# A fused attention and gated-convolution kernel: the order of all its steps and loads written anew

## The chip, the core and the metric

The kernel runs on one core of one Trainium2 chip. A core has five engines that run side by side, each working through its own instructions strictly in the order in which the program issued them: TensorE (PE in the profile: matrix products and transposes into PSUM), VectorE (DVE), ScalarE (ACT, the exponentials, ReLU and tanh), GpSimd (POOL) and SyncE (SP). SP computes nothing here; it issues nearly all transfers, and they go through one hardware queue that is served by the core's 16 DMA engines. Engines wait for each other, and for transfers, through semaphores. The metric is the device time in microseconds (us) of one execution, the median of several runs.

## What is computed

Eight sequences of 576 positions go through an attention with 8 heads of width 64 and a decay, and the result through a feed-forward network with a gate made from a convolution over three neighbouring positions. All inputs and the output are float32.

```python
def _attn_ref(q, k, v, f):                      # q, k, v: (8, 8, 576, 64), f: (8, 8, 576)
    scores = scale * np.matmul(q, k.transpose(0, 1, 3, 2))
    cum = np.cumsum(np.log(np.clip(f, 0.0001, 1.0)), axis=-1)
    decay = cum[:, :, :, None] - cum[:, :, None, :]
    scores = np.where(causal, -1000000000.0, scores + decay)
    attn = np.exp(scores - np.max(scores, axis=-1, keepdims=True))
    attn = attn / (np.sum(attn, axis=-1, keepdims=True) + 1e-09)
    return np.matmul(attn, v)

def _moe_ref(x, w_in, conv_w, w_out):           # x: (8, 576, 512), d_ff = 1024
    h = np.maximum(x @ w_in, 0.0)
    conv_out = sum(conv_w[k] * hp[:, k:k + S, :] for k in range(3))
    return (h * (1.0 / (1.0 + np.exp(-conv_out)))) @ w_out
```

## The kernel before

The work is cut into steps with short names. Attention goes by **blocks** of four heads, so that there are 16 blocks, 0 to 15, two for each sequence; the feed-forward part goes by sequence, 0 to 7. In the names below `hb` is a block, `b` a sequence, `i` a pair of heads (two in a block, `i` = 2`hb` and 2`hb`+1), and `ff` one of eight slices of 128 hidden columns.

Loads, all issued by SP unless said otherwise:
- `ld0.*` and `ld1.*` bring q and k of blocks 0 and 1 in plainly; TensorE then transposes them (`tp`, nine 128x128 transposes each, L166) and ACT or DVE copies them from PSUM into place (`cl0`, `cl1`, L172 and L174).
- `q{hb}.0` and `q{hb}.1` bring q and k of every later block in with a transposing transfer each (L180), into one of four places in turn (`qk_85` holds blocks 0, 4, 8, 12, `qk_86` blocks 1, 5, 9, 13, and so on). Up to block 7 DVE then clears the rows that carry the decay (`cl{hb}.side`, L186), and `rw{hb}` (L204, L205; SP or ACT issues it) copies these rows in from `image`, which `ki` has written from the sums of log f (`dca`, `dcl`, `dcs`, `dck`). From block 8 on `fi{hb}` fills them.
- `v{b}.0` to `v{b}.4` bring v of a sequence (L211); `va{hb}.0` and `va{hb}.1` cast it to 16 bits for a block (L219, L221; POOL, ACT or DVE). `va{hb}.0` needs `v{b}.0` to `v{b}.3`.
- `wi0` to `wi3` and `wo0` to `wo3` bring the weights (L518); `wic`, `woc` cast them.

Attention: `sd{i}`, `so{i}.0`, `so{i}.1` and `st{hb}` are the scores (L314; the mask is added on TensorE by L322 in blocks 0 to 7), `ed`, `eo` and `et` their exponentials on ACT (L355, L372, L334). `pv{hb}.0` and `pv{hb}.1` multiply by v (L391, L396), `n` and `m` divide by the sum on DVE (L405, L407), `t` transposes the result on TensorE (L416) and `tx` copies it (L419). In block 0 the decay is added by two more products for each score (L317, L319).

Feed-forward: `f{b}.{ff}` is the first product (L431), `r` its ReLU on ACT (L442), `c` and `d` the convolution on DVE (L448, L450), `a` the tanh on ACT (L453), `g` the gate on DVE (L460), `o{b}.{c}` the second product (L476), `e` the copy out of PSUM and `s` the store (L503 and its neighbours; L498 in the last sequence).

PSUM is four banks of 128x1024, handed out in turn: a step on TensorE that takes a bank waits until the step that empties the bank's last content has ended. So each score product waits for an exponential some steps back.

What sets the order is a table, `ORDER`: a string with the name of every step (and of the engine where a step can run on more than one, as in `va2.0@ACT`). The program issues the steps in that order, so it fixes the order on each engine and on the transfer queue; the scheduler moves nothing. A step's resources (PSUM banks, buffers) go first come, first served along the same table. Eight semaphores are used in turn for transfers, so that the ninth transfer is issued only when the first of the nine has arrived.

## Time and profile before

| | |
|---|---|
| median of three runs | 247.25 us (245.05, 247.81 and 247.25) |
| span of the profiled execution, first to last instruction | 244.7 us |
| TensorE busy | 228.6 us, 93% of the span |
| ScalarE busy | 206.8 us, 85% |
| VectorE busy | 205.5 us, 84% |
| GpSimd busy | 51.9 us, 21% |
| moved by the DMA engines | 49.68 MB, mean 203 GB/s |

The profile page gives for the profiled execution its span alone; what lies around a span (the start and the end of an execution) is in the runs' times and not in it, so the median stands 2.55 us above the span. "Busy" counts overlapping instructions of an engine once. Two tenths-rows of the page show that TensorE is full in nearly every fortieth of the span but the first ten and the last, and that the DMA engines are full until about five sixths of it.

### The profile page before, as it was taken

How to read it: one execution, taken by the hardware profiler on the slowest of the kernel's cores; microseconds unless marked ns; L12 is line 12 of the kernel's file. 1: busy time of each engine (PE TensorE's matmuls, PEld its weight loads, DVE VectorE, ACT ScalarE, POOL GpSimd, SP SyncE). 2: the span in 40 equal slices, each digit the busy share in tenths (PEclk: the TensorE clock that was granted, in tenths of full speed). 3: DMA queues.
4: the chain of work that ended last, by engine and by line, in shares of the span. 5: the costliest groups of instructions: out<-in, count | busy, mean ns of one | idle time of the engine just before them, and what ended most of it. 6: DMA issues, size and time to landing. Idle time of an engine off the chain costs nothing.

```text
span 244.7 us, 6393 instructions
## 1 busy us (share of the span) xinstructions
PE 228.6 (93%) x2627; PEld 146.1 (60%) x2627; DVE 205.5 (84%) x324; ACT 206.8 (85%) x278; POOL 51.9 (21%) x77
## 2 busy tenths in 40 slices
...
GB/s 189 334 169 250 278 184 189 223 198 306 196 216 196 169 182 220 238 268 251 224 212 274 194 198 269 270 102 196 265 198 227 195 209 4 106 173 77 171 85 216
DMA packets 120424, 49.68 MB, mean 203 GB/s; under 512 B 109879, under 2 KB 110647, under 8 KB 120395
## 3 DMA queue, kind: packets, MB, share of 16 engines
...
q10 hardware_dynamic: 322, 0.47, 0.6%
q8 instruction: 20, 0.33, 0.6%
...
HBM read 21.11 MB, written 10.17 MB: 128 GB/s over the span
## 4 chain that ended last, share of the span: by engine, by line
PE 81%; DMA 5%; DVE 5%; ACT 5%; issue 1%; SPq 1%; ACTq 0%; DVEq 0%
PE ps L476 26%; PE ps L431 23%; PE ps L314 15%; PE ps L391 7%; DMA qk<-image 3%; PE ps L322 3%; PE ps L396 3%; DMA u<-in_f_dram 2%; PE ps L416 2%; ACT qk L172 2%; DVE u L450 2%; DVE u L448 1%; ACT ht L442 1%; ACT pp L372 1%; PE ps L317 1%
## 5 line engine op out<-in xcount | busy, mean ns | idle before, releaser
L431 PE MATMUL ps<-xt,w_in_f 128*128 128x512 f16 (+1 forms) x512 | 71.0, 288 | 0.4 <-DVE xt L419 0.4
L372 ACT ACTIVATE pp<-ps 128x1024 f16<-128x1024 f32 x64 | 64.8, 1032 | 3.7 <-PE ps L314 2.3
L476 PE MATMUL ps<-w_out_f,hg 128*128 128x512 f16 x288 | 66.8, 379 | 0.0
L314 PE MATMUL ps<-qk 128*128 128x128 bf16 (+2 forms) x576 | 63.9, 241 | 2.1 <-DMA qk<-image 0.9
L448 DVE SCALAR_TENSOR_TENSOR u<-ht,cwt 128x576 f32<-128x576 f16 x64 | 52.4, 832 | 4.4 <-ACT ht L442 4.2
L450 DVE SCALAR_TENSOR_TENSOR u<-ht,cwt,u 128x576 f32<-128x576 f16 x64 | 53.9, 856 | 0.5
L453 ACT ACTIVATE hg<-u,cw 128x576 f16<-128x576 f32 x64 | 48.7, 782 | 6.1 <-DVE u L450 6.0
L431 PEld LDWEIGHTS <-w_in_f 128*128 128x128 f16 x512 | 34.7, 99 | 29.4 <-issue 1.3
L314 PEld LDWEIGHTS <-qk 128*128 128x128 bf16 x576 | 39.4, 98 | 19.2 <-issue 2.5
L442 ACT ACTIVATE ht<-ps 128x576 f16<-128x576 f32 x64 | 41.0, 664 | 6.4 <-PE ps L431 2.8
L476 PEld LDWEIGHTS <-hg 128*128 128x128 f16 x288 | 26.9, 98 | 28.9
L460 DVE SCALAR_TENSOR_TENSOR hg<-hg,ht 128x576 f16<-128x576 f16 x51 | 38.6, 767 | 0.6 <-ACT hg L453 0.5
L358 POOL TENSOR_SCALAR_AFFINE_SELECT pp<-pd 128x1024 f16<-128x1024 f32 x16 | 19.7, 1244 | 53.6 <-ACT pd L355 53.6
L391 PE MATMUL ps<-va,pp 128*128 128x65 f16 x640 | 25.3, 194 | 1.7 <-DVE va L219 1.7
L391 PEld LDWEIGHTS <-pp 128*128 128x128 f16 x640 | 23.0, 98 | 4.2 <-DVE va L219 1.9
L407 DVE TENSOR_TENSOR xm<-ps,rc 128x896 f16<-128x896 f32 (+1 forms) x32 | 23.9, 751 | 0.5
L355 ACT ACTIVATE pp<-ps 128x1024 f16<-128x1024 f32 x16 | 16.6, 1038 | 5.2 <-PE ps L314 4.0
L219 POOL CAST va<-vf 128x1024 f16<-128x1024 f32 x8 | 10.0, 1247 | 34.3 <-PE ps L314 18.8
L355 ACT ACTIVATE pd<-ps 128x1024 f32<-128x1024 f32 x16 | 16.2, 1023 | 1.2 <-PE ps L314 0.5
L405 DVE RECIPROCAL rc<-ps 128x14 f32<-128x14 f32 (+1 forms) x32 | 6.6, 207 | 10.2 <-PE ps L396 4.9
L322 PE MATMUL ps<-mask,ident 128*128 128x512 bf16 (+1 forms) x40 | 14.4, 364 | 0.4 <-ACT pp L372 0.3
L481 ACT COPY ob<-ps 128x1024 f32<-128x1024 f32 (+1 forms) x14 | 12.9, 918 | 0.3 <-issue 0.2
...
## 6 DMA issues: line engine op xcount, KB each, us to landing
...
```

Of the source, the lines that this page charges most:

```text
L314: nc.tensor.matmul(o, tk[:, h * S + k0:h * S + k0 + 128], tq[:, h * S + q0:h * S + q0 + n], start=first, stop=last and not by_matmul(hb, h))
L355: nc.scalar.activation(o, ps_of(f"sd{i}").rearrange("p (s c) -> p s c", s=2), AF.Exp, scale=SCALE)
L372: nc.scalar.activation(pair(i)[:, s, 512:1536], ps_of(f"so{i}.{s}"), AF.Exp, scale=SCALE)
L391: nc.tensor.matmul(ps[:, c:c + D + 1], block(hb, h, m, n), va[:, h, m, 0:D + 1], start=(m == 0), stop=(m == n))
L407: nc.vector.tensor_tensor(xm[:, CUT * D * u:CUT * D * u + nj * k * D].rearrange("p (j x d) -> p j x d", x=k, d=D), got[:, :, :, 0:D], r.un ...
L431: nc.tensor.matmul(ps[:, t0:t1], w_in_f16[:, cc, 128 * ff:128 * (ff + 1)], xt[:, cc // 2, x:x + t1 - t0], start=(cc == 0), stop=(cc == NCC ...
L442: nc.scalar.activation(ht_of(b, ff)[:, 2:2 + S], ps_of(f"f{b}.{ff}")[:, 0:S], AF.Relu, scale=1.0 if (b, ff) in LATE else 0.5)
L448: nc.vector.scalar_tensor_tensor(u, ht[:, 1:1 + S], cwt[:, ff, 0:1], ht[:, 2:2 + S], op0=ALU.mult, op1=ALU.add)
L450: nc.vector.scalar_tensor_tensor(u, ht[:, 3:3 + S], cwt[:, ff, 1:2], u, op0=ALU.mult, op1=ALU.add)
L453: nc.scalar.activation(hg_of(b, ff), u_t[slot[f"c{b}.{ff}", "u"]], AF.Sigmoid if (b, ff) in LATE else AF.Tanh, scale=cw[:, ff, 1:2])
L460: nc.vector.scalar_tensor_tensor(hv, hv, 1.0, ht_of(b, ff)[:, 2:2 + S], op0=ALU.add, op1=ALU.mult)
L476: nc.tensor.matmul(ps[:, 512 * j:512 * (j + 1)], w, w_out_f16[:, ff, :], start=(ff == 0), stop=(ff == NFF - 1))
```

## The change

One string is replaced: `ORDER`. The names in it are the same 1056 steps; their order is new on every engine and on the transfer queue, and some steps that may run on either of several engines have another one. The rest of the program is untouched (its lines move down by 51, since the new table is broken into lines).

```diff
 ORDER = """
-dca cw ld0 ld1 ld0.0.0 tp0.0.0 dcl ld0.1.0 ld0.0.1 tp0.0.1 tp0.1.0 v0.0 ld0.1.1 ld1.0.1 ld1.0.0 dcs dck v0.1 ...
+ld0 v0.0 dca q2.0 ld1 dcl q2.1 ld0.0.0 ld0.0.1 tp0.0.0 cl0.0.0@ACT tp0.0.1 ld1.0.0 dcs cl2.1 ld1.0.1 dck cl0.0.1@DVE
+ki@ACT cw v0.3 tp1.0.0 cl1.0.0@ACT ld0.1.0 tp1.0.1 tp1.1.0 v0.2 ld0.1.1 cwt v1.0 wi1 v0.4 cl1.0.1@DVE tp1.1.1 v1.4 sd0
...
 """
```

Steps with another engine: `ki` and `rw3` go to ACT's queue, `rw4` and `rw5` to SP's; `va2.0` goes from DVE to ACT, `va3.0`, `va3.1` and `va4.0` from ACT to POOL, `va5.0` and `va6.0` from POOL to DVE, and more than twenty further casts, copies and stores change places in the same way.

Three places of the order matter below. The first is the start of SP's queue. Before, q and k of block 0 come first (`hg` is where the plain loads land):

```order
L159 DMA hg<-in_q_dram 128x576 x2
L159 DMA hg<-in_k_dram 128x576
L211 DMA vf_89<-in_v_dram 128x8x64
L159 DMA hg<-in_k_dram 128x576
L159 DMA hg<-in_k_dram 128x2x576
L159 DMA hg<-in_q_dram 128x2x576
L211 DMA vf_89<-in_v_dram 128x8x64 x3
```

Now a load of v and both transposing loads of block 2 (`qk_87`) stand ahead of them, and the plain loads of block 1 (128x2x576) stand ahead of the second half of block 0's:

```order
L262 DMA vf_89<-in_v_dram 128x8x64
L231 DMA_TRANSPOSE qk_87<-in_q_dram 128x2304
L231 DMA_TRANSPOSE qk_87<-in_k_dram 128x2304
L210 DMA hg<-in_q_dram 128x576
L210 DMA hg<-in_k_dram 128x576
L210 DMA hg<-in_q_dram 128x2x576
L210 DMA hg<-in_k_dram 128x2x576
L262 DMA vf_89<-in_v_dram 128x8x64
L210 DMA hg<-in_q_dram 128x576
```

So the first scores of block 0 have more in front of them on the queue, and block 2 is there early. The second place is ScalarE between the exponentials of block 1 and the first ReLU. Before it has no cast there (`pp` and `pt` are exponentials, `ht` is a ReLU):

```order
L372 ACTIVATE pp_99<-ps_131 128x1024
L355 ACTIVATE pp_100<-ps_131 128x2x512
L442 ACTIVATE ht_115<-ps_130 128x576
L442 ACTIVATE ht_116<-ps_132 128x576
L372 ACTIVATE pp_100<-ps_129 128x1024
```

Now a cast of v (`va2.0`, from `vf_90`, which waits for the four large loads of sequence 1's v) and the issue of block 3's row copies (`rw3`) stand ahead of two exponentials of block 2 and of the first ReLU:

```order
L385 ACTIVATE pt_103<-ps_131 128x256
L270 CAST va_94<-vf_90 128x4x4x64
L423 ACTIVATE pp_99<-ps_130 128x1024
L255 DMA qk_88<-image 1x2304
L256 DMA qk_88<-image 2x2304
L423 ACTIVATE pp_100<-ps_129 128x1024
L493 ACTIVATE ht_115<-ps_131 128x576
L423 ACTIVATE pp_100<-ps_130 128x1024
```

Before, that cast was on VectorE, behind the first convolutions. The third place is SP's queue around blocks 4 to 6 (`qk_85` is block 4, `qk_86` block 5, `qk_87` block 6). Before, the loads of block 6 follow three weight loads and all of sequence 2's v:

```order
L180 DMA_TRANSPOSE qk_86<-in_q_dram 128x2304
L180 DMA_TRANSPOSE qk_86<-in_k_dram 128x2304
L518 DMA ob_125<-in_moe_w_out_dram 128x2x512
L518 DMA ob_126<-in_moe_w_out_dram 128x2x512
L518 DMA ob_127<-in_moe_w_out_dram 128x2x512
L211 DMA vf_89<-in_v_dram 128x8x64 x2
L211 DMA vf_89<-in_v_dram 64x8x64
L211 DMA vf_89<-in_v_dram 128x8x64 x2
L518 DMA ob_128<-in_moe_w_out_dram 128x2x512
L180 DMA_TRANSPOSE qk_87<-in_q_dram 128x2304
L180 DMA_TRANSPOSE qk_87<-in_k_dram 128x2304
```

Now they stand between the two loads of block 5, and the row copies of block 6 ahead of those of block 5:

```order
L231 DMA_TRANSPOSE qk_86<-in_q_dram 128x2304
L262 DMA vf_89<-in_v_dram 128x8x64 x2
L255 DMA qk_85<-image 1x2304
L256 DMA qk_85<-image 2x2304
L231 DMA_TRANSPOSE qk_87<-in_q_dram 128x2304
L231 DMA_TRANSPOSE qk_87<-in_k_dram 128x2304
L231 DMA_TRANSPOSE qk_86<-in_k_dram 128x2304
L262 DMA vf_89<-in_v_dram 128x8x64
L255 DMA qk_87<-image 1x2304
L256 DMA qk_87<-image 2x2304
```

TensorE's order follows: the first score product of block 6 (`sd13`) now stands ahead of that of block 5 (`sd11`), both ahead of the first sequence's second product, and far earlier among TensorE's steps than before.

More of the change, by code (lines that the diff above doesn't have):

```diff
@@ new lines @@
+ld0 v0.0 dca q2.0 ld1 dcl q2.1 ld0.0.0 ld0.0.1 tp0.0.0 cl0.0.0@ACT tp0.0.1 ld1.0.0 dcs cl2.1 ld1.0.1 dck cl0.0.1@DVE
+ki@ACT cw v0.3 tp1.0.0 cl1.0.0@ACT ld0.1.0 tp1.0.1 tp1.1.0 v0.2 ld0.1.1 cwt v1.0 wi1 v0.4 cl1.0.1@DVE tp1.1.1 v1.4 sd0
+cl1.1.1@DVE cl2.0 tp0.1.0 tp0.1.1 cl1.1.0@ACT so0.0 cl0.1.0@ACT rw1@SP wi2 ed0 rw2@SP v0.1 q3.1 so0.1 q3.0 cl0.1.1@DVE
+va0.0@POOL va0.1@DVE wic2@POOL cl3.1 v1.1 wi0 sd1 v1.2 so1.1 eo0.0 ed1 va1.0@DVE sd2 eo1.1 va1.1@POOL wi3 st0 eo0.1
+ed2 so1.0 so2.1 et0 sd3 v1.3 eo1.0 wic1@POOL eo2.1 ed3 so2.0 sd5 ed5 cl3.0 eo2.0 pv0.0 so3.1 pv0.1 wo1 n0.0 q4.0 m0.0
@@ new lines @@
+so3.0 eo3.1 n0.1 m0.1 wic0@POOL va3.0@POOL sd4 st1 eo3.0 pv1.0 et1 ed4 n1.0 st2 so5.0 pv1.1 et2 t0 m1.0 n1.1 m1.1
+va2.0@ACT t1 so4.1 eo5.0 tx0@DVE rw3@ACT so4.0 tx1@DVE q4.1 q5.0 cl4.0 eo4.1 f0.0 f0.1 f0.2 r0.0 wic3@POOL c0.0 eo4.0
+v2.0 d0.0 h0 r0.1 r0.2 f0.3 woc1@POOL cl4.1 a0.0 so5.1 c0.2 r0.3 eo5.1 f0.4 c0.3 va2.1@POOL r0.4 st3 sd6 et3 v2.2
+rw4@SP va3.1@POOL d0.3 c0.1 q6.0 ed6 sd7 c0.4 pv2.0 a0.3 ed7 so6.1 d0.4 f0.5 so6.0 n2.0 eo6.1 g0.0 m2.0 d0.1 pv2.1
+so7.0 r0.5 f0.6 n2.1 q6.1 a0.4 cl5.0 eo6.0 eo7.0 q5.1 so7.1 a0.1 m2.1 sd8 cl6.0 g0.4 d0.2 eo7.1 v2.1 r0.6 st4 cl6.1
@@ new lines @@
+pv3.0 so8.0 a0.2 et4 c0.5 ed8 n3.0 rw6@SP sd9 v2.3 g0.2 eo8.0 m3.0 wo2 pv3.1 so8.1 ed9 n3.1 d0.5 f0.7 eo8.1 m3.1 v3.0
+cl5.1 t2 r0.7 so9.0 t3 tx2@ACT c0.6 tx3@DVE c0.7 sd13 rw5@SP so9.1 g0.3 a0.5 eo9.0 eo9.1 ed13 g0.1 f1.0 v2.4
+va4.0@POOL sd11 wo0 d0.6 pv4.0 so11.1 r1.0 woc0@POOL f1.1 g0.5 n4.0 woc2@POOL ed11 sd10 eo11.1 m4.0 st6 f1.2 a0.6 v3.3
+wo3 c1.0 r1.1 va4.1@POOL d0.7 et6 ed10 c1.1 r1.2 pv4.1 n4.1 d1.0 h1 g0.6 woc3@DVE so10.1 q7.1 so11.0 d1.1 eo10.1 f1.3
+f1.4 eo11.0 r1.3 a0.7 m4.1 va5.0@DVE va5.1@ACT a1.1 q7.0 so10.0 g0.7 r1.4 a1.0 q8.0 cl7.0 g1.1 v3.2 cl7.1 v4.0 f1.5
@@ new lines @@
+r1.5 o0.0 t4 c1.4 c1.5 o0.1 c1.2 tx4@ACT d1.5 sd12 st5 v3.1 d1.4 eo10.0 ed12 et5 e0.0@ACT pv5.0 a1.4 n5.0 d1.2 rw7@SP
+m5.0 so13.0 pv5.1 f1.6 n5.1 eo13.0 g1.0 q8.1 m5.1 v4.4 f1.7 g1.4 v3.4 va6.0@DVE q9.1 st7 c1.3 a1.2 r1.6 d1.3 et7 r1.7
+sd14 so13.1 c1.6 c1.7 a1.5 so12.0 d1.7 eo12.0 o0.2 eo13.1 t5 so14.1 a1.3 zc g1.2 ed14 o0.3 tx5@DVE f2.0 f2.1 d1.6 q9.0
+eo14.1 e0.1@ACT r2.0 fi8 va7.0@DVE a1.6 so12.1 f2.2 g1.5 a1.7 r2.1 g1.3 g1.6 f2.3 va6.1@DVE sd15 r2.2 eo12.1 v4.3 v4.1
+va7.1@DVE r2.3 so15.0 fi9 v4.2 c2.1 c2.0 d2.1 so15.1 ed15 c2.2 eo15.0 f2.4 d2.0 g1.7 pv6.0 eo15.1 sd16 s0.1 n6.0 m6.0
```

33 lines of the change are left out of this document (32 added, 1 removed).

## The prediction

> **What bounds the kernel now.** I read the windows first (columns: stretch, its length, busy time and count of each engine, TensorE clock, DMA share, GB/s), then the end of the chain of waits (start, length, what).
>
> ```profile
> 0.00:60.00 60.00, 47.99 (x647) 36.16 (x647) 39.23 (x76) 43.60 (x52) 14.64 (x41) 0.97 1.03 232
> 60.00:240.70 180.70, 180.66 (x1992) 109.93 (x1986) 165.85 (x248) 162.88 (x226) 37.29 (x37) 1.00 0.88 194
> ...
> 228.58 12.10 PE ps L476 x56
> 240.71 0.38 ACT ob L492
> 241.11 0.42 DVE u L492
> ```
>
> From 60 us to the last product at 240.7 TensorE is busy for 180.66 of 180.70 us; what can be won lies in the first 60 us (12.0 us idle) and in the 4.0 us from 240.7 to the span's end at 244.7. To compare two orders I need the work itself, back to back. These rows of the chain and of the timeline give it:
>
> ```profile
> 15.78 0.50 PE ps L166 x9
> 195.77 1.96 PE ps L431 x16
> 197.73 0.44 PE ps L314 x4
> 202.10 1.00 PE ps L391 x32
> 206.07 0.44 PE ps L396 x20
> 212.11 3.45 PE ps L476 x16
> ...
> 45.06 0.38 PE L322 MATMUL ps<-mask,ident 128*128 128x512 bf16 x1
> 45.50 0.38 PE L322 MATMUL ps<-mask,ident 128*128 128x512 bf16 x1
> ```
>
> A transpose step is 0.50, `f` 0.98, `o` 1.73, `so` 0.44 (1.31 in block 0, three products for one), `pv.0` 1.00, `pv.1` 0.80 with its changes of shape, `sd` 0.88 with the mask (half of it from 45.06 to 45.50), 0.45 without it and 1.78 in block 0, `st` 0.1 to 0.45, `cw` 0.9. Over all steps: f 62.7, o 62.1, so 31.4, sd 23.1, st 2.9, pv 28.8, transposes 9.5, cw 0.9: about 221.6 us. I call **lag** the start of a step less the work ahead of it (these prices, added along TensorE's steps in the table); the span is 221.6 + last lag + 4.0.
>
> ```profile
> 7.15 0.98 PE L296 MATMUL ps<-one,pd 3*128 3x3 f32 x8 [7.15 <-DMA pd<-in_moe_conv_w_dram]
> 12.22 0.58 PE L322 MATMUL ps<-mask,ident 128*128 128x512 bf16 x1
> 37.30 0.65 PE L431 MATMUL ps<-xt,w_in_f 128*128 128x512 f16 x4
> 61.02 0.78 PE L416 MATMUL ps<-ident,xm 128*128 128x128 f16 x8
> ...
> PE ps L391 <- DVE va L219: 1.7, 1, 1.7
> ...
> 48.00:50.00 2.00, 0.33 (x4) 0.05 (x3) 2.00 (x4) 2.00 (x3) 0.00 (x0) 1.00 1.25 115
> 50.00:54.00 4.00, 4.00 (x44) 2.67 (x45) 3.62 (x7) 4.00 (x6) 0.00 (x0) 0.57 1.13 240
> ```
>
> Before, the lag is 9.3 at the first score (12.2 - 2.9 of work), 12.6 at `f0.0` (37.3 - 24.7), 18.3 at `t3` (61.0 - 42.75) and 19.1 at 228.58 (work ahead 221.6 - 12.1). The 5.7 us between `f0.0` and `t3` are 1.7 for a cast on VectorE (`va2.0`), 1.7 for half clock (0.57 over 4 us is 1.7 lost, right after that wait), and 2.3 of small waits.
>
> **The transfer queue.** It is what a new order has to live with. The SP rows give the time to issue a transposing load, which is the time in which the queue takes it:
>
> ```profile
> L180 SPq DMA_TRANSPOSE qk<-in_k_dram x14: 2011/2847/3962, 15.3 to 175.2; - x14
> 94.34 4.45 SPq L180 DMA_TRANSPOSE qk<-in_q_dram x2
> ...
> q8 instruction: 20, 0.33, 0.6%
> ...
> 29.00:30.00 1.00, 1.00 (x14) 0.75 (x13) 0.00 (x0) 1.00 (x2) 0.49 (x1) 1.00 1.63 297
> 30.00:31.00 1.00, 1.00 (x24) 0.81 (x24) 0.00 (x0) 1.00 (x2) 0.32 (x1) 1.00 1.91 104
> 31.00:32.00 1.00, 0.67 (x21) 0.33 (x17) 0.57 (x2) 1.00 (x2) 0.72 (x1) 1.00 0.21 44
> ...
> 9.00:10.00 1.00, 1.00 (x12) 1.00 (x11) 0.97 (x2) 0.99 (x2) 0.00 (x0) 1.00 1.06 396
> 13.00:14.00 1.00, 1.00 (x19) 0.88 (x17) 0.76 (x1) 0.37 (x1) 0.00 (x0) 1.00 1.23 211
> 24.00:28.00 4.00, 3.55 (x61) 2.83 (x61) 2.04 (x3) 2.18 (x4) 2.02 (x2) 1.00 0.86 266
> ```
>
> Two that were not stopped took 4.45, 2.2 each; the median is 2.85. There were 20 instruction fetches of 16 KB, one for some 128 of TensorE's 2627 products. Where one meets a transposing load, the queue falls from 297 to 104 and 44 GB/s: about 1.6 us lost in 30 to 32. Rates for the rest: plain q and k 396 GB/s (0.75 us for 0.295 MB, 1.5 for 0.59), v 211 (1.24 for 0.262 MB), weights 266 (1.97 for 0.524 MB).
>
> The Trainium skill, "Runtime: NRT & Kernel Launch", Instruction fetch mechanics, says that instructions come in blocks of 16 KiB through a queue of the sequencer's own and that this is mostly hidden. By that rule every transposing load would cost the 2.0 us of the shortest. The trace agrees on the blocks and not on the hiding: 44 GB/s.
>
> **The change, part by part.** All instructions are kept, so the 221.6 stay; an engine that is given another cast pays about 1 us off the path, since ScalarE and VectorE are busy for 163 and 166 of the 180.7 us.
>
> (1) The first score. The queue now holds, before the second load of block 1: v 1.24, two transposing loads 4.4, f 0.75, two plain loads 1.5, two large ones 3.0; with 1.8 to the first data and 1.0 to arrive (estimates, from the 2.1 us between the end of an SP issue at 20.90 and the VectorE step that waited for it), `ld0.0.0` is there at 9.9, `ld1.0.1` at 13.7. TensorE does `tp0.0.0` from 9.9 (0.93 each while the clock is low, as in the rows from 8.06), then `tp0.0.1`, `cw`, `tp1.0.0`, `tp1.0.1`, `tp1.1.0` until 14.7. `tp1.1.1` needs the bank that ScalarE empties with `cl1.0.0`, and ahead of that ScalarE has `cl0.0.0` and now the three issues of `ki`:
>
> ```profile
> 13.48 1.82 SPq L281 DMA_DIRECT2D image<-kc  x3
> L172 ACT ACTIVATE qk<-ps,lim 128x1152 uint16<-128x1152 uint16 x5 | 6.3, 1307 | 0.0
> L186 DVE TENSOR_SCALAR qk<-qk,lim 128x2304 uint16<-128x2304 uint16 x12 | 10.4, 879 | 1.1 <-DMA qk<-in_q_dram 1.1
> L407 DVE TENSOR_TENSOR xm<-ps,rc 128x896 f16<-128x896 f32 x16 | 17.4, 1087 | 0.3
> L219 ACT CAST va<-vf 128x1024 f16<-128x1024 f32 x4 | 4.3, 1068 | 0.0
> L372 ACT ACTIVATE pp<-ps 128x1024 f16<-128x1024 f32 x64 | 64.8, 1032 | 3.7 <-PE ps L314 2.3 <-PE ps L319 1.4
> ```
>
> 10.9 + 1.3 + 1.8 + 1.3 = 15.3, the turn until 15.8: `sd0` at 15.8 with 3.9 of work ahead, lag 11.9. Price: +2.6.
>
> (2) `f0.0`. On VectorE `cl3.0` stands ahead of `n0.0`, so block 0's division waits for block 3's load. Queue up to `q3.0`: 1.8 + 6.0 plain + 0.75 f + 7.45 v (five large, two half) + 3.95 (two weights) + 0.6 row copies + 8.8 (four transposing) + 2.1 (two fetches, one on a transposing load) = 31.45, there at 32.4. Then `cl3.0` 0.88, `n0.0` and `m0.0` 1.3, and behind that bank `sd4`, `pv1.0`, `so5.0`, `pv1.1`, its division, `t1`, `so4.1`: 39.9. ScalarE meanwhile stands at `va2.0`, which needs `v1.3`: 31.45 + three v 3.7 + two weights 3.95 + a fetch 0.5 + 1.0 = 40.6; cast 1.07, `eo5.0` 1.03, `so4.0` 0.44: `f0.0` at 43.1, work ahead 25.8, lag 17.3 (before 12.6). If `v1.3` were in time, 40.3 and 14.5. I take the first: every term is a row's. Price: +4.7, with the 2.6 of (1) in it.
>
> (3) From there to `t3`. The cast that cost 1.7 is done by then, the half clock is not certain (below), and of the 2.3 of small waits I keep half: block 3's `so7.0` still waits for `m2.0`, as its like did before. Lag 17.3 + 1.1 = 18.4, against 18.3.
>
> (4) Block 6 and 5. `sd11` needs the row copies of block 5; its work ahead is 48.0, before 50.6. The queue up to them: 1.8 + 6.0 + 0.75 + 17.4 (v: 13 large, two half) + 11.8 (six weights) + 1.5 (five row copies) + ten transposing loads at 2.2 = 22.0 + fetches 3.6 (one on a transposing load, four beside: by counting 128 products for each fetch, they now fall on weights and v) = 64.85, there at 65.9: the lag cannot be under 17.9. At the median of 2.85, which has its fetches in it, 22.8; at 2.0, 15.9. I take 2.2, the rows without a stop, because the counted fetches lie elsewhere. It ends just before (3) does, so it adds nothing, but it leaves no slack. Blocks 7 and 8 come out alike (17 to 18).
>
> (5) The rest. Before, the lag grew by 0.8 after `t3`; I keep that. At the end the last chunk is now copied whole (0.59 instead of two halves of 0.4) and stored whole: +0.2.
>
> **Sum.** Lag 18.4 + 0.8 = 19.2; 221.6 + 19.2 + 4.2 = 245.0, against 244.7 of the profiled span. With the 2.55 us by which the median stands above the span: 247.5.
>
> **Rivals.** *Faster: the loads come in time.* For it: transposing loads that are not stopped take 2.0 to 2.2, and in (2) the lag without the wait for `v1.3` is 14.5. With 2.0 and no fetch on a transposing load the limit of (4) is 14.8; 14.5 + 0.6 of small waits is 15.1, 3.2 under before's 18.3: 247.25 - 3.2 + 0.2 = 244.2, and down to 243 if the small waits go too. It decides if `v1.3` is there before 38 and block 5's rows before 63.5. Against it: the queue was never that fast for ten such loads in a row.
>
> *Slower: TensorE waits for block 5, 6, 7 or 8.* The queue keeps the median 2.85 of before, since a fetch that comes a few us later than planned falls on a transposing load after all (so the change would not do what it is made for). The lag at `sd11` is then 22.8, 4.5 above before: 247.25 + 4.5 + 0.2 = 252.0. It decides if block 5's rows come after 68.6 (lag 20.6). For it: the first needs of blocks 5, 6, 7 and 8 come 2.6, 21.7, 6.3 and 8.1 us of work earlier than before, so what slack the queue had is spent.
>
> *Half clock.* Before, a wait of 1.7 us in 48 to 50 is followed by 0.57 of the clock. The wait at `so4.0` in (2) is of that size, so 1.7 us may come back: time 249.2, inside my case. The Trainium skill, "TensorE: Matmul & The Clock Gate", Part 1, says that the clock falls to half after an idle window of about 3.4 us and stays there until a busy one; here a window that was only about half idle was enough.
>
> **Chances.** Within 1% (244.8 to 249.7; about what a measurement here can tell from no change): 0.42, my own case with its price of 2.1 to 2.5 for a transposing load, with or without half clock; its own range is 245 to 249.7. Faster by more: 0.33, the first rival, 243 to 244.8. Slower by more: 0.25. Leaving out one in ten at each end: 243.0 to 251.5.
>
> **What would show it.** (1) `sd0` near 15.8 and three DMA issues on ScalarE between its copies; wrong if it starts by 13. (2) A VectorE row that waits for `q3` ahead of block 0's division and a ScalarE cast (L270) that waits for v for 2 us or more; wrong if `f0.0` starts before 40. (3) No TensorE wait for a VectorE cast near 48. (4) GB/s falling below 100 in the windows of weights or v and not of transposing loads; waits of TensorE for `qk<-image` between 60 and 110 mean the slower rival. Wrong in sum if TensorE's idle time before 60 us is under 9 or if it idles by more than 2 us after 70.

## The result, and the profile after

| | before | after |
|---|---|---|
| median of the runs of this comparison | 246.64 us (four, 245.05 to 247.81) | 252.99 us (four, 252.71 to 254.18) |
| ratio | | 1.028, 95% interval 1.022 to 1.034 |
| span of the profiled execution | 244.7 us | 251.0 us |
| TensorE busy | 228.6 us | 227.8 us |
| lag (as the prediction defines it) at `sd0`, `f0.0`, `t3`, the last products | 9.3, 12.6, 18.3, 19.1 | 17.0, 18.7, 22.2, 24.0 |
| TensorE's last product to the span's end | 4.0 us | 5.1 us |

The changed kernel is 2.8% slower by the ratio, which is estimated from the single runs and is not the quotient of the two medians. Here and below, medians leave out executions that took over 1.5% longer than the fastest of their kernel. TensorE does the same work, and waits more. The windows of the changed kernel (the columns as before; the second ends with TensorE's last product at 245.9) say where:

```profile
0.00:60.00 60.00, 43.81 (x575) 33.57 (x576) 35.51 (x68) 38.10 (x45) 13.44 (x41) 1.00 1.10 227
60.00:245.90 185.90, 184.04 (x2056) 112.44 (x2053) 172.04 (x258) 167.16 (x233) 38.49 (x36) 1.00 0.87 188
```

In the first 60 us TensorE idles 16.2 us (12.0 before), in the rest 1.9 (none before). Most of the first part is one wait at the very start. The timeline of the changed kernel there (start, length, engine or its queue, line, operation; in brackets the idle time ahead and what ended it):

```profile
0.80 0.61 ACTq L275 DMA_DIRECT2D u<-in_f_dram  x1
0.80 0.46 SPq L262 DMA_DIRECT2D vf<-in_v_dram  x1
1.32 3.88 SPq L231 DMA_TRANSPOSE qk<-in_q_dram  x1
5.25 4.60 SPq L231 DMA_TRANSPOSE qk<-in_k_dram  x1
8.85 0.46 DVE L585 TENSOR_SCALAR u<-u 128x576 f32<-128x576 f32 x1 [4.58 <-DMA u<-in_f_dram]
9.89 0.58 SPq L210 DMA_DIRECT2D hg<-in_q_dram  x1
13.16 2.10 PE L217 MATMUL ps<-ident_b,hg 128*128 128x128 bf16 x18 [13.16 <-DVE kc L326]
18.04 3.06 PE L217 MATMUL ps<-ident_b,hg 128*128 128x128 bf16 x27 [0.77 <-DMA hg<-in_k_dram]
20.90 0.47 PE L373 MATMUL ps<-mask,ident 128*128 128x512 bf16 x1
```

The plain loads of block 0 are issued only at 9.89, when both transposing loads of block 2 have been taken; TensorE's first transpose starts at 13.16 (the row names a cast as the releaser, but what came is `hg`, issued at 9.89; the cast is no input of a transpose), the first score at 20.90. The transposes ahead of it follow each other at 0.107 us a product (27 in 2.86 us from 18.04) where later ones take 0.055. By the records of single packets the first transposing load ran from 3.7 to 9.0, 5.3 us. The windows show what the queue did in that time, in the changed kernel:

```profile
3.00:4.00 1.00, 0.00 (x0) 0.00 (x0) 1.00 (x5) 0.36 (x1) 1.00 (x11) 1.00 1.30 301
4.00:5.00 1.00, 0.00 (x0) 0.00 (x0) 0.27 (x2) 0.00 (x0) 0.88 (x13) 1.00 1.25 180
5.00:6.00 1.00, 0.00 (x0) 0.00 (x0) 0.00 (x0) 0.00 (x0) 0.78 (x4) 1.00 1.35 150
6.00:7.00 1.00, 0.00 (x0) 0.00 (x0) 0.00 (x0) 0.00 (x0) 0.41 (x2) 1.00 1.12 121
7.00:8.00 1.00, 0.00 (x0) 0.00 (x0) 0.00 (x0) 0.00 (x0) 0.00 (x0) 1.00 1.17 102
```

The DMA engines are full (last column but one) and move 102 to 180 GB/s: the transposing load and the transfers of f, which come through ScalarE's queue, go at once, and both are slow (f's first use at 8.85, 7.16 before). The second difference is spread out. These are the waits of VectorE for transposing loads, first of the changed kernel:

```profile
DVE qk L237 <- DMA qk<-in_k_dram: 5.6, 3, 4.8
DVE qk L237 <- DMA qk<-in_q_dram: 3.8, 3, 3.3
```

and of the kernel before:

```profile
DVE qk L186 <- DMA qk<-in_q_dram: 1.1, 1, 1.1
```

Six times, 9.4 us in all, VectorE stands at a clear of decay rows (`cl`) with other work behind it; before, once, 1.1 us. In the changed kernel this costs TensorE little: the largest wait of TensorE that follows from one is 1.2 us, at block 3's first score (51.4). I take it that the late start had already used up most of that time. The loads themselves are no faster than before (time to issue, least, median and most; then the fetches):

```profile
L231 SPq DMA_TRANSPOSE qk<-in_q_dram x14: 1968/3008/4765, 1.3 to 173.7; - x14
L231 SPq DMA_TRANSPOSE qk<-in_k_dram x14: 2702/3360/6394, 5.3 to 177.0; - x14
...
q8 instruction: 20, 0.33, 0.6%
```

and in the kernel before, beside the row for k that the prediction shows (median 2847):

```profile
L180 SPq DMA_TRANSPOSE qk<-in_q_dram x14: 2054/2860/6792, 18.5 to 179.1; - x14
```

By the packets, 11 of the 28 transposing loads of q and k run beside one of the 20 fetches for 0.1 us or more, and 8 did before; counting those that a fetch only touches it is 14 and 12. So the changed order does not do what it was planned for. And a fetch costs less than the prediction thought, which had 1.6 us from one dip. Counted from the last packet of the transfer ahead to the last of the load itself, loads beside a fetch take 3.3 us and the others 2.5, the collided one left out (before 3.5 and 2.6); over the traces of all versions it is 3.2 and 2.5. The price of 2.2 is low for both.

The Trainium skill, "Runtime: NRT & Kernel Launch", Instruction fetch mechanics, has the cost of a fetch "mostly hidden". That sentence is about the engine whose instructions are fetched; for a transfer beside a fetch the traces here give about 0.7 us, less than the prediction's one dip to 44 GB/s and more than nothing.

### The profile page after: what moved, and what is told of

Its sections match the earlier page's. It is cut to its first block, busy times and chain, and to the rows that moved or that the text cites. A ratio compares the mean times of both kernels' runs of the same rounds, so it can differ in the third digit from the quotient of the medians.

```text
span 251.0 us, 6385 instructions
## 1 busy us (share of the span) xinstructions
PE 227.8 (91%) x2627; PEld 146.0 (58%) x2627; DVE 207.6 (83%) x325; ACT 205.8 (82%) x277; POOL 51.9 (21%) x77
## 4 chain that ended last, share of the span: by engine, by line
PE 64%; DMA 13%; SPq 10%; ACT 4%; issue 3%; POOL 2%; DVE 1%; POOLq 0%; ACTq 0%; DVEq 0%
PE ps L527 24%; PE ps L482 19%; PE ps L365 11%; SPq L231 6%; DMA vf<-in_v_dram 6%; PE ps L442 6%; DMA qk<-in_q_dram 3%; DMA hg<-in_q_dram 3%; PE ps L447 2%; ACT pp L423 2%; DMA qk<-image 1%; PE ps L467 1%; POOL w_out_f L577 1%; ACT hg L504 1%; SPq L262 1%
## 5 line engine op out<-in xcount | busy, mean ns | idle before, releaser
L482 PE MATMUL ps<-xt,w_in_f 128*128 128x512 f16 (+1 forms) x512 | 69.6, 286 | 0.2 <-DVE xm L458 0.2
L365 PE MATMUL ps<-qk 128*128 128x128 bf16 (+2 forms) x576 | 64.2, 240 | 1.0 <-ACT pp L423 0.5
L499 DVE SCALAR_TENSOR_TENSOR u<-ht,cwt 128x576 f32<-128x576 f16 x64 | 53.8, 858 | 1.1 <-ACT ht L493 1.0
L501 DVE SCALAR_TENSOR_TENSOR u<-ht,cwt,u 128x576 f32<-128x576 f16 x64 | 53.2, 841 | 0.6
L409 POOL TENSOR_SCALAR_AFFINE_SELECT pp<-pd 128x1024 f16<-128x1024 f32 x16 | 21.9, 1371 | 70.3 <-ACT pd L406 70.2
L458 DVE TENSOR_TENSOR xm<-ps,rc 128x896 f16<-128x896 f32 (+1 forms) x32 | 24.1, 753 | 0.6
L217 PE MATMUL ps<-ident_b,hg 128*128 128x128 bf16 x72 | 7.5, 289 | 13.9 <-DVE kc L326 13.2
L237 DVE TENSOR_SCALAR qk<-qk,lim 128x2304 uint16<-128x2304 uint16 x12 | 11.3, 943 | 9.4 <-DMA qk<-in_k_dram 5.6
L270 POOL CAST va<-vf 128x1024 f16<-128x1024 f32 x7 | 7.3, 1045 | 54.7 <-DMA vf<-in_v_dram 54.7
L406 ACT ACTIVATE pp<-ps 128x1024 f16<-128x1024 f32 x16 | 16.5, 1038 | 1.9 <-PE ps L370 1.8
```

Source lines behind the costliest of these rows:

```text
L365: nc.tensor.matmul(o, tk[:, h * S + k0:h * S + k0 + 128], tq[:, h * S + q0:h * S + q0 + n], start=first, stop=last and not by_matmul(hb, h))
L406: nc.scalar.activation(o, ps_of(f"sd{i}").rearrange("p (s c) -> p s c", s=2), AF.Exp, scale=SCALE)
L458: nc.vector.tensor_tensor(xm[:, CUT * D * u:CUT * D * u + nj * k * D].rearrange("p (j x d) -> p j x d", x=k, d=D), got[:, :, :, 0:D], r.un ...
L482: nc.tensor.matmul(ps[:, t0:t1], w_in_f16[:, cc, 128 * ff:128 * (ff + 1)], xt[:, cc // 2, x:x + t1 - t0], start=(cc == 0), stop=(cc == NCC ...
L499: nc.vector.scalar_tensor_tensor(u, ht[:, 1:1 + S], cwt[:, ff, 0:1], ht[:, 2:2 + S], op0=ALU.mult, op1=ALU.add)
L501: nc.vector.scalar_tensor_tensor(u, ht[:, 3:3 + S], cwt[:, ff, 1:2], u, op0=ALU.mult, op1=ALU.add)
```

## The experiments

Each kernel is a new order of the same steps (the lines of ORDER are shown; "..." leaves steps out), and computes the full result. All were run beside the kernel before, whose median was 245.3 to 246.3. The lags are those of one profiled execution each. How far such a lag can be trusted shows in x16's row: up to `f7.7` that order is the changed kernel's, and its lags differ from it by 0.2 to 1.8. So a single lag under 2 us apart proves nothing by itself.

| run | lag `sd0` | `f0.0` | `sd11` | `o6.0` | median us | ratio to before (95%) |
|---|---|---|---|---|---|---|
| before | 9.3 | 12.6 | 18.6 | 18.9 | 246.6 | |
| after | 17.0 | 18.7 | 22.2 | 24.0 | 253.0 | 1.028 (1.022 to 1.034) |
| x1_q2_behind | 16.8 | 20.3 | 22.4 | 25.5 | 254.6 | 1.035 (1.028 to 1.041) |
| x2_q2_first | 11.8 | 14.0 | 20.4 | 20.8 | 248.1 | 1.009 (1.006 to 1.013) |
| x3_old_start | 9.4 | 22.7 | 24.9 | 27.0 | 256.1 | 1.038 (1.032 to 1.044) |
| x4_new_start | 16.5 | 21.6 | 28.7 | 29.0 | 256.3 | 1.040 (1.035 to 1.045) |
| x5_q2_cl2_behind | - | - | - | - | 254.2 | 1.035 (1.029 to 1.042) |
| x6_old_start_cl2_late | 9.5 | 21.4 | 24.1 | 26.3 | 254.4 | 1.034 (1.027 to 1.041) |
| x7_v00_behind_q2 | 14.8 | 17.6 | 20.2 | 21.4 | 250.8 | 1.022 (1.016 to 1.028) |
| x8_old_v00_q2_first | 15.4 | 17.3 | 22.6 | 23.0 | 250.3 | 1.019 (1.015 to 1.024) |
| x9_q3_v13_waits_away | 14.9 | 15.9 | 20.7 | 21.9 | 252.0 | 1.025 (1.021 to 1.030) |
| x10_one_q2_behind | 12.1 | 14.6 | 22.5 | 25.7 | 252.8 | 1.030 (1.024 to 1.035) |
| x12_old_v1_before_q4 | 9.3 | 12.0 | 19.2 | 19.5 | 247.2 | 1.007 (1.005 to 1.010) |
| x13_cl4_behind | 11.8 | 14.2 | 21.4 | 23.8 | 252.5 | 1.028 (1.023 to 1.032) |
| x14_after_cl4_behind | 17.0 | 18.4 | 21.0 | 21.7 | 252.7 | 1.032 (1.026 to 1.038) |
| x15_old_va20_pool | 9.3 | 12.0 | 18.7 | 19.1 | 247.1 | 1.005 (1.002 to 1.007) |
| x16_after_old_tail | 17.4 | 19.4 | 22.0 | 25.8 | 252.9 | 1.029 (1.023 to 1.036) |
| x17_after_wo1_behind | 17.9 | 20.1 | 22.5 | 26.8 | 253.6 | 1.026 (1.021 to 1.031) |
| x18_early_wo_behind | 12.0 | 14.4 | 19.2 | 23.6 | 253.2 | 1.026 (1.022 to 1.030) |
| x19_va41_first_old_tail | 11.9 | 14.3 | 18.4 | 23.4 | 251.6 | 1.026 (1.022 to 1.030) |

(x5 has no lags; its median is of two executions, as is that of x16.)

**The start alone.** Two kernels take one part of the change into the kernel before: x2 puts block 2's two transposing loads at the queue's head, x8 the same with one load of v ahead of them, as the change has it.

```diff
-dca cw ld0 ld1 ld0.0.0 ... v0.0 ... q2.1 ... q2.0
+dca cw ld0 q2.0 q2.1 ld1 ld0.0.0 ... v0.0
+dca cw ld0 v0.0 q2.0 q2.1 ld1 ld0.0.0
```

> The kernel before with one thing of the change done alone: the two transposing loads of block 2 at the head of the transfer queue, ahead of all plain loads. Theory A: the first of the two takes about 5 us beside the transfers of f, the first transposes start at 12 to 13 (8 to 9 before), the first score at 16 to 18 (12.2 before), and the time is 250 to 253. Theory B: the start is late by as much, but there is slack behind it (small waits that vanish, loads that are early), and the time is within 1% of before, under 249.

> The kernel before with the first load of v and then both transposing loads of block 2 at the head of the queue (the run that had the transposing loads alone at the head gave 248.1, its first one took 3.1 us). Theory A, collision: with v ahead of it the first transposing load runs beside f's transfers, takes 5 us or more, the first transposes start at 13 (10.2 in that run, 8.1 before) and, the lag being carried, the time is 251 (250 to 252). Rival: v ahead costs only its own 1.2 us, the first transposes start at 11.4, time 249.3.

In x2 the first load took 3.1 us and not 5, so the first transposes are late by 2.1 us only, and the time is 248.1, 0.9% slower: theory B's figure, but not its reason: of the 2.5 us of lag at `sd0` 1.9 are still there at the end, and the median is 2.1 above that of the kernel before in the same comparison (246.0). x8 came out as theory A has it (250.3). The timeline of x2, where f's transfers (first row) and the first transposing load are issued together, at 0.80 (the second transposing load is shown):

```profile
0.80 0.61 ACTq L275 DMA_DIRECT2D u<-in_f_dram  x1
3.11 3.71 SPq L231 DMA_TRANSPOSE qk<-in_k_dram  x1
6.90 0.46 DVE L585 TENSOR_SCALAR u<-u 128x576 f32<-128x576 f32 x1 [2.63 <-DMA u<-in_f_dram]
10.18 1.14 PE L217 MATMUL ps<-ident_b,hg 128*128 128x128 bf16 x9 [2.13 <-DMA hg<-in_q_dram]
```

and of x8:

```profile
4.83 5.39 SPq L231 DMA_TRANSPOSE qk<-in_k_dram  x1
10.40 0.46 DVE L585 TENSOR_SCALAR u<-u 128x576 f32<-128x576 f32 x1 [6.13 <-DMA u<-in_f_dram]
13.62 1.14 PE L217 MATMUL ps<-ident_b,hg 128*128 128x128 bf16 x9 [2.47 <-DMA hg<-in_q_dram]
```

One load of v, 1.2 us of queue, moves the first transposes by 3.4 us and the use of f by 3.5, and the time by 2.2 (the intervals do not overlap). In x2's windows the queue moves 257 and 298 GB/s where it moved 180 and 150 above:

```profile
4.00:5.00 1.00, 0.00 (x0) 0.00 (x0) 0.27 (x2) 0.00 (x0) 0.88 (x13) 1.00 1.28 257
5.00:6.00 1.00, 0.00 (x0) 0.00 (x0) 0.00 (x0) 0.00 (x0) 0.78 (x4) 1.00 1.21 298
```

So it is shown that a load of v at the head makes the transposing load behind it slow, and what that costs. By the packets, f's transfers begin first in that case (2.8 in the changed kernel, the transposing load 3.7) and second in x2 (3.2, the load 2.2). It is the same in the other traces: with v ahead the first transposing load takes 4.9 to 5.5 us (the changed kernel, x4, x8, x14, x16, x17), at the very head 3.1 to 3.4 (x2, x7, x9, x10). The load of v alone is not enough: in the changed kernel a load of block 3 follows a load of v directly (issued at 26.93 and 26.18) and takes 2.5. That it is f's transfers which slow it is the reading that is left; no run moved them. x7 undoes that order in the changed kernel, by the same load of v:

```diff
-ld0 v0.0 dca q2.0 ld1 dcl q2.1 ld0.0.0
+ld0 dca q2.0 ld1 dcl q2.1 v0.0 ld0.0.0
```

> The changed kernel with one load moved by two places: the first load of v goes behind the two transposing loads of block 2 instead of ahead of them, so that the same bytes stand ahead of block 0's plain loads, but the transposing load starts before the transfers of f. If the 5.3 us of that load come from running beside f's transfers at an unlucky moment, it takes 3.1 to 3.4 as in the run that had it at the very head, the first transposes start at 11.2 to 11.8 (13.2), and with a carried lag the time falls by 1.5 to 2, to 251. If they come from the mere presence of f's transfers, the load takes about 5 us again and the time stays within 0.5 of 253.

```profile
0.80 2.23 SPq L231 DMA_TRANSPOSE qk<-in_q_dram  x1
7.05 0.46 DVE L585 TENSOR_SCALAR u<-u 128x576 f32<-128x576 f32 x1 [2.78 <-DMA u<-in_f_dram]
12.06 2.36 PE L217 MATMUL ps<-ident_b,hg 128*128 128x128 bf16 x18 [12.06 <-DMA hg<-in_q_dram]
```

The load takes 3.3 us by its packets, f is there 1.8 us earlier, the first score 2.2 earlier (18.7), and the median is 250.8: as expected but for the first transposes (12.1, expected by 11.8), though the intervals of the ratios (1.016 to 1.028 and 1.022 to 1.034) overlap. It is the fastest version of the new order that was found, and still 2.2% slower than before.

**The whole start, and why it wins nothing.** x1, x3, x4, x5 and x6 undo or exchange the start as a whole.

```diff
-ld0 v0.0 dca q2.0 ld1 dcl q2.1 ld0.0.0 ... ld0.1.1 cwt
+ld0 v0.0 dca ld1 dcl ld0.0.0 ... ld0.1.1 q2.0 q2.1 cl2.1 cwt
```

> The changed kernel with one thing undone: the two transposing loads of block 2 go behind the last plain load of blocks 0 and 1, and the step that clears block 2's decay rows with them. Everything else is as changed. Theory A (the start): the two transposing loads ahead of block 0's plain loads hold up the queue (5.3 us for the first, since it runs beside the transfers of f on ScalarE's queue), all later work is late by it, and it is never won back. By A the first transposes start by 8.5 (13.2 in the changed kernel), the first score by 15.5 (20.9), block 2's transposing loads take 2.9 us or less each, and the time falls from 253 to 247 to 249. Theory B (the rest): the later order, with the loads of blocks 5 to 8 close behind each other, costs the time whatever the start does; then the first score comes as early as by A, but the lag has grown to 21 or more by block 5's scores, and the time stays at 251.5 or above.

> The steps up to the first score in the order of the kernel before, all other steps in the changed order. Theory A: the first score at 12 to 13, a lag of about 9.5 there, and up to 7.7 us come off the 253: 245 to 248. Theory B: the first score is as early, but TensorE then waits for the loads of blocks 3 to 8 and the time is 250 or more.

> The reverse: the steps up to the first score in the changed order, all other steps in the order of the kernel before. Theory A: the first score near 20.9, a lag of 17 there, and the time is 251 to 255. Theory B: the old order behind the start wins part of it back, and the time is 247 to 250.

> The run with block 2's transposing loads behind the plain ones had left a wait of its own: VectorE stood for 7.0 us at the clear of block 2's rows, ahead of the copies of block 1 and of the convolution weights. Here both clears of block 2 and its row copies go behind the last copy of block 0 as well; all else is as changed. Theory A (the start is late by the loads put first, and the lag is carried to the end): first transposes at 6.8, first score at 15 (lag 11 against 17.0 in the changed kernel), time 247 (246 to 248.5). Theory B (the rest of the new order has a limit of its own, the loads of blocks 3 to 8 and of sequence 1's v): the first score is at 15 too, but by f0.0 or block 5's scores the lag is back at 20 or above, time 250 or more.

> The steps up to the first score in the order of before, the rest in the changed order, with the clears of block 2 and its row copies behind the last copy of block 0, so that VectorE no longer stands at them. Theory A: lag 9.4 at the first score, and little more is lost than in the changed kernel from there on (7.0 to the end): time 245 to 247. Theory B: TensorE waits for loads behind the first score, and the lag is 20 or above by block 5's scores: 250 or more.

All came out slower than the changed kernel's 253.0 (254.2 to 256.3). Theory B's open bounds allow that for x1, x3, x5 and x6, but neither theory had foreseen it. x3 shows why; with the old start, VectorE then meets the clear of block 2 early:

```profile
21.01 0.88 DVE L237 TENSOR_SCALAR qk<-qk,lim 128x2304 uint16<-128x2304 uint16 x1 [8.53 <-DMA qk<-in_k_dram]
23.33 1.12 PE L217 MATMUL ps<-ident_b,hg 128*128 128x128 bf16 x9 [5.85 <-DVE qk L225]
```

VectorE stands 8.5 us at a clear with a copy of block 1 behind it, and TensorE 5.9 us for that copy. What follows runs at a lower clock: the mean granted clock of this execution is 0.977, against 0.998 in the changed kernel. x1 has the same wait (7.0 us), and in x6, where the clear goes behind, block 2's row copies then come behind two more transposing loads on SP's queue (issued at 33.7), and TensorE waits 3.4 us for them. x4, the new start with the old rest, has no wait over 2 us and loses 12.5 us from the first score to the end (before: 9.6), in small waits and one stretch at half clock, as before has one; the old rest wins nothing back. So in these five a start could not be exchanged by itself: the rest of each order is fitted to its own.

x9 and x10 avoid new waits of that kind. x9 takes x7, puts the second step's two waits elsewhere and issues the last store from ScalarE (all versions from x9 to x18 built on it keep that; the span's end stays 5.2 to 5.4 us behind TensorE's last product); x10 moves one of block 2's loads back as well.

```diff
-cl3.0 eo2.0 ... n0.0 ... m0.1 ... va2.0@ACT t1 ... r0.2
+eo2.0 ... n0.0 ... m0.1 cl3.0 ... t1 ... r0.2 va2.0@ACT
...
-s7.0@SP
+s7.0@ACT
...
-ld0 dca q2.0 ld1 ... ld0.1.1 cwt
+ld0 dca ld1 ... ld0.1.1 q2.0 cwt
```

> The run with the first load of v behind block 2's loads (250.8), with three steps put elsewhere: VectorE's clear of block 3's rows behind block 0's division instead of ahead of it, ScalarE's cast of v (va2.0) behind the first ReLUs instead of ahead of the last exponentials of block 2, and the very last store on ScalarE's queue instead of SP's. This tests the second step of the prediction. If those waits are the limit between the first score and f0.0, the 1.3 us at block 2's fifth score and the 0.6 at so4.0 go, the end is 0.9 shorter, and the time is 248.0 (247.4 to 248.8). If another wait stands right behind them (block 3's row copies come later now), TensorE loses the same before block 3's scores and only the end's 0.9 is won: 249.9.

> The run above with one transposing load of block 2 more moved: q2.0 goes behind the last plain load, q2.1 stays at the head (VectorE needs it early), so that no engine gets a new wait at the start. Theory A (start lag is carried): the plain loads come 2.2 to 2.8 us earlier, the first score at 16.2 (18.7), and the time is 2.2 to 2.8 under the run above: 245.5. Theory B (the loads of block 3 and of sequence 1's v limit f0.0): the lag at f0.0 falls by under 1, time 247.3 or above.

In x9 the waits go and the lag at `f0.0` falls from 17.6 to 15.9, but 2.2 us are lost at block 3's first score instead; the time does not fall (the rival's mechanism, though its 249.9 was not reached). In x10 the first score comes at 16.0, `f0.0` at 40.3 (44.4 in the changed kernel), and then:

```profile
46.77 0.88 DVE L237 TENSOR_SCALAR qk<-qk,lim 128x2304 uint16<-128x2304 uint16 x1 [6.12 <-DMA qk<-in_q_dram]
47.56 0.81 DVE L499 SCALAR_TENSOR_TENSOR u<-ht,cwt 128x576 f32<-128x576 f16 x1
49.33 0.77 ACT L504 ACTIVATE hg<-u,cw 128x576 f16<-128x576 f32 x1 [4.24 <-DVE u L501]
50.01 0.63 ACT L493 ACTIVATE ht<-ps 128x576 f16<-128x576 f32 x1
50.69 0.59 PE L373 MATMUL ps<-mask,ident 128*128 128x512 bf16 x1 [4.63 <-ACT ht L493]
```

Read it downwards: VectorE waits for block 4's load at a clear, the convolution behind it is late, then ScalarE's tanh, then the ReLU behind the tanh, then TensorE's bank. The start's gain is gone, and the wait is paid twice: behind it TensorE runs at half clock for some us. The mean clock of the first 60 us (third number from the end) was 1.00 in the changed kernel and is 0.94 here, which is 3.6 us of full clock:

```profile
0.00:60.00 60.00, 45.59 (x570) 35.26 (x571) 34.43 (x68) 37.72 (x44) 13.49 (x41) 0.94 1.06 229
```

In the changed kernel the same clear starts at 47.44: block 4's load comes when the queue gets to it, whenever the start was.

**Is it the clears, or the queue?** x13 puts the clears of block 4 behind the convolutions in x10, x14 does that alone in the changed kernel.

```diff
-cl4.0 eo4.1 f0.0 ... c0.0 ... cl4.1 a0.0 ... c0.3 va2.1@POOL
+eo4.1 f0.0 ... c0.0 ... a0.0 ... c0.3 cl4.0 cl4.1 va2.1@POOL
```

> The run with the earliest start of the changed order (first score at 16.0, lag 14.6 at f0.0, yet 252.8) lost 4.8 us before block 3's first score: VectorE stood for 6.1 us at the clear of block 4's rows, waiting for its load, with sequence 0's first convolution behind it; the tanh, the next ReLU on ScalarE and TensorE's bank followed. Here both clears of block 4 go behind the fourth convolution step; all else is as in that run. Theory D (what the new order loses are clears on VectorE that stand ahead of work and wait for a load that is late): the 4.8 falls to under 1, the lag at block 3's first score is 15 to 16, and the time 248 to 249.5. Theory B (the loads themselves are the limit): block 4's rows come no earlier, TensorE waits for them at block 4's scores instead, the lag is 20 there all the same, time 251.5 or above.

> The changed kernel with only the clears of block 4 moved behind the fourth convolution step. There the same wait cost TensorE 1.4 us at block 3's first score. By theory D that goes and is carried: 251.6 (251.0 to 252.2). By theory B a load ends the wait a little later: 253 as the changed kernel.

In x13 the 4.8 us at block 3's first score are gone (lag 14.6 there), as theory D has it, and 3.5 us come back five steps later, at the second of the clears:

```profile
50.31 0.88 DVE L237 TENSOR_SCALAR qk<-qk,lim 128x2304 uint16<-128x2304 uint16 x1 [2.22 <-DMA qk<-in_k_dram]
51.95 0.78 ACT L504 ACTIVATE hg<-u,cw 128x576 f16<-128x576 f32 x1 [3.40 <-DVE u L501]
53.68 1.00 PE L365 MATMUL ps<-qk 128*128 128x64 bf16 x4 [3.36 <-ACT pp L406]
```

In x13, too, half clock follows that wait (0.97 over the first 60 us, 1.8 us lost). x14 is inconclusive: its profiled execution took 250.4, its median is 252.7 and the changed kernel's 253.0. x17 and x18 then take loads out of the queue that nothing needs soon: wo1 from ahead of block 4's loads (x17, in the changed kernel), wo1 and wo2 (x18, in x13; the cast of wo1 goes ahead of that of wo0).

```diff
-v1.3 ... wo1 ... q4.0 ... wo2 ... v2.4 ... wo0
+v1.3 ... q4.0 ... v2.4 wo1 wo2 ... wo0
```

> The changed kernel with one load of 0.5 MB that nothing needs soon (wo1, a weight of the second product, first used 40 us later) moved from ahead of block 4's loads to behind sequence 2's v, with its cast. The queue's load of it took 2.0 us. If the queue is the limit (the slower rival of the prediction, with about 3 us for a transposing load), blocks 4, 6 and 5 come 2 us earlier, VectorE waits less at the clears of block 4, the 1.4 us at block 3's first score go, and the time is 251.3 (250.5 to 252). If the start alone sets the lag, the time stays within 0.5 of 253.

> The run with the earlier start and the clears of block 4 behind the convolutions (252.5; it lost 3.5 us at so6.0 behind the second of these clears, which still waited 2.2 us for block 4's second load), with two weight loads (wo1 and wo2, 2 us each) moved from ahead of the loads of blocks 4 to 6 to behind sequence 2's v. If the queue is the limit, block 4's second load is there 2 us earlier, block 5's rows 4 us earlier, the 3.5 shrinks to 1.5 or less, the lag at block 5's score falls from 21.4 to 18 or 19 and the time to 249.5 (248.5 to 250.5). If it is not, another wait takes its place and the time stays at 252 or above.

x17 won nothing (its start happened to be 1 us later than the changed kernel's). In x18 the queue did what was expected: the last row copies of block 5 are issued at 64.2 (67.3 in the changed kernel), the 3.5 us shrink to 0.8, and the lag at block 5's score is 19.2 against 21.4 in x13 (the clock is 0.97 over the first 60 us here too). The time stayed at 253.2, for TensorE met this:

```profile
76.38 0.22 PE L447 MATMUL ps<-va,pt 128*64 128x65 f16 x2 [3.15 <-POOL va L272]
```

GpSimd's cast of v stood behind casts of the weights that had been put later. x19 puts that cast first, and the steps behind `f7.7` in the order of before, which x16 does alone.

```diff
-va4.0@POOL ... woc0@POOL ... woc2@POOL ... va4.1@POOL
+va4.0@POOL va4.1@POOL ... woc1@POOL woc0@POOL ... woc2@POOL
```

> The run above did reach block 5's scores with a lag of 19.2 (22.2 in the changed kernel), and then lost 3.3 us at so10.1: GpSimd's cast of the last rows of v for block 4 (va4.1) stood behind the casts of weights whose loads had been put later. Here that cast goes ahead of them, and the steps behind the last first product have the order of before (span's end 3.5 us behind TensorE's last product instead of 5.1). If what the new order loses are casts and clears that stand ahead of work and wait for loads, the 3.3 go: lag 20 to 21 at the last products, time 248.5 (247.5 to 249.7). If every wait that is taken away is only followed by the next one, the lag is back at 22.5 or more by the last products, and the time is 250.5 or above.

> The changed kernel with all steps behind the last first product (f7.7) in the order and on the engines of before. It tests the fifth step: the time from TensorE's last product to the span's end, 5.1 in the changed kernel against 4.0 before. If it is the order of the last copies and stores, it is 4.0 here and the time 251.8. If it is the queue's backlog from earlier stores, it stays at 5.1 and the time at 253.

In x19 block 4 passes with a lag of 18.4, and the next clear, of block 7, takes it back:

```profile
82.12 0.88 DVE L237 TENSOR_SCALAR qk<-qk,lim 128x2304 uint16<-128x2304 uint16 x1 [3.66 <-DMA qk<-in_q_dram]
83.76 0.65 ACT L493 ACTIVATE ht<-ps 128x576 f16<-128x576 f32 x1 [3.89 <-DVE hg L511]
84.46 0.58 PE L373 MATMUL ps<-mask,ident 128*128 128x512 bf16 x1 [2.81 <-ACT ht L493]
...
60.00:120.00 60.00, 56.62 (x696) 37.18 (x694) 54.62 (x83) 54.41 (x74) 10.32 (x9) 0.97 1.05 222
```

The last row is the window from 60 to 120: a clock of 0.97 over 60 us is 1.8 us lost, on top of the wait of 2.8. Lag 23.4 at the end, 251.6 us: the expectation's second case. x16 shows the last term in its profile, 3.5 us from TensorE's last product (248.2) to the span's end (251.7) instead of 5.1, but not in its time (252.9, two runs), where 1.6 us are within the scatter.

**The old order's own wait.** x12 and x15 tried to win the 1.7 us and the half clock of before.

```diff
-t1 q4.1 v1.0 ... v1.1 ... rw3@SP ... v1.3 v1.2 ... va2.0@DVE
+t1 v1.0 ... v1.1 v1.3 v1.2 ... rw3@SP q4.1 ... va2.0@DVE
...
-q4.0 va2.0@DVE
+q4.0 va2.0@POOL
```

> The kernel before with one piece of queue order changed: the first load of block 4 (and its clear) goes behind sequence 1's v, since TensorE had waited 1.7 us for the cast of that v while block 4 is needed only 15 us later. If that wait and the half clock behind it (1.7 us lost) are a pure loss, the lag at t3 falls from 18.3 to 15 to 16.6 and the time to 243 (242.3 to 244.6), under both kernels. If something else waits at the same place (the convolution steps on VectorE, block 4's loads in turn), the time stays within 0.5 of before's 245.5 to 246.5.

> The kernel before with one cast (va2.0) on GpSimd instead of VectorE, at the same place of the table. There it stood behind four convolution steps on a VectorE that was full, and TensorE waited 1.7 us for it, with half clock behind it (1.7 more). If both are a pure loss: lag at t3 15 to 16.6 (18.3), time 243 (242.3 to 244.6), less than either kernel. If v comes too late for GpSimd or the next step on VectorE takes the wait over, the time stays within 0.5 of 245.6.

Both are slower than before, by 0.7% and 0.5%. In x12 the cast still ends the wait, since it stands behind convolutions on a full VectorE and v was not what it waited for. In x15 the cast is early, and TensorE waits 1.2 us at the same place for a ReLU and then 1.4 for an exponential; the half clock only moves. The windows of x15 (TensorE's clock is the third number from the end):

```profile
50.00:52.00 2.00, 1.61 (x14) 0.77 (x11) 2.00 (x5) 2.00 (x3) 0.00 (x0) 1.00 1.20 256
52.00:54.00 2.00, 0.39 (x5) 0.28 (x5) 2.00 (x3) 2.00 (x4) 0.00 (x0) 1.00 1.14 215
54.00:56.00 2.00, 1.87 (x19) 1.36 (x20) 1.86 (x4) 1.59 (x6) 0.00 (x0) 0.50 0.91 236
```

VectorE is busy throughout, which points to it, and not to the place of one cast, as the limit in that stretch; no run relieved it. No version beat the kernel before.

## Why the prediction was wrong, step by step

The forecast sum was a span of 245.0; it was 251.0. By lags the 6.0 us are: step (1) +5.1, from there to `t3` -1.3 (5.2 lost where 6.5 was forecast), the rest +1.0 (1.8 for 0.8), the end +1.2 (251.0 - 221.6 - 24.0 = 5.4 for 4.2).

- **(1), the first score: wrong, and the step that failed.** Forecast 15.8, measured 20.9. The term is "two transposing loads 4.4": the first took 5.3 and the second 2.3, so `ld0.0.0` came at 13.2 for 9.9 (+3.3). The price of 2.2 was read from two loads in mid-kernel beside which the other queues moved almost nothing; here f came through another queue at the same time, and the sum had put f's 0.75 us beside them as if the two only added. `ld1.0.1` lost 1.0 more, and from there to the score the three transposes took 2.86, at 0.107 us a product, where the prediction had 2.1 (1.5 of work at full pace and 0.6 of waiting). The three issues of `ki` on ScalarE are there (1.9 us), but not on the path. x2 and x8 show the slow load and what it costs; that f is what it meets is read from the packets.
- **(2), `f0.0`: the waits are right, their cost is not.** VectorE waits 4.8 us for block 3's load at `cl3` ahead of block 0's division, and ScalarE's cast of v waits for v, but 0.7 and not 2. `f0.0` was at 44.4 for 43.1, and that the two are near is luck: 5.1 too much in (1) and 3.7 too little here. Since everything was already late, these waits cost 1.7 in lag and not 5.4; x7, with an earlier start, pays 2.8.
- **(3): right.** No TensorE wait for that cast, and no half clock: from the end of the slow transposes at 21 on, the clock's windows read 1.00 to past the last product.
- **(4), blocks 5 and 6: wrong in the price again.** The row copies of block 5 were there at 69.6 by their packets, forecast 65.9. Ten transposing loads up to there took 3.07 each with the collision in it, 2.8 without it; not 2.2. The reason given, that the counted fetches lie elsewhere, failed twice: no fewer loads meet a fetch than before, and loads that meet none take 2.5 to 2.6.
- **(5)**: small, but low: 1.0 in the rest and 1.2 at the end. x16's profile puts the end down to the order of the last copies and stores.

**The rivals.** The slower one gave 252.0 and the condition that block 5's rows come after 68.6; they came at 69.6, and the time was 253.0. Yet TensorE did not wait for those rows: its start had made it as late, and its one wait for row copies, 0.5 us, is at 106. So the rival's number came near for another reason than its own. What the runs point to is two limits of nearly the same height. One is the late start (x2, x8, x7). The other is the queue at its true pace, and TensorE meets it mostly not at the scores but through VectorE's and GpSimd's clears and casts, which stand at a late load with the work that TensorE needs behind them. With the start repaired in part (x10, x13, x18, x19: lag 12 at `sd0`) the time stays at 251.6 to 253.2. Each of these four loses 1.8 to 3.6 us to half clock behind a wait, which the changed kernel and x7 do not have (1.00 over the first 120 us); so the later waits weigh more there than their length, and how much of the 251.6 to 253.2 is the queue and how much the clock was not separated. The faster rival fell with the same price. Half clock did not come in the changed kernel.

The Trainium skill, "DMA: Bandwidth & Descriptors", Queues, rings and completion order, says that a DMA engine takes turns between its queues, one packet of descriptors at a time. The trace agrees that the two queues ran at once. Taking turns alone would cost the load f's 0.29 MB; it lost 2 to 3 us, and the sum of both fell to 102 GB/s. That loss the page doesn't give.

**What stays open.** Why transposing loads without a fetch take anything from 1.7 to 3.6 us, counted as above over the traces, was not found; no kernel was run in which they alone move, and none with f's transfers elsewhere. Nor is it shown that the waits end with block 7: x19 was the last step, and no version of the new order came under 250.8.
